# Moving scale chains, statistics, inversions and negations behind an emptied matmul bank in a fused attention and SwiGLU kernel

## The chip, the cores and the metric

One NeuronCore of a Trainium2 chip. Its engines are named as in the profile: PE (TensorE matmul; PEld is its weight load), DVE (VectorE), ACT (ScalarE), POOL (GpSimd) and SP (SyncE, which here issues most of the DMAs). The metric is the device time of one execution in microseconds (us), lower is better. For the kernel before, three runs gave a median of 825.03 us (824.76 to 825.77).

## The reference

```
xn = layernorm(x)                                   # x is 2048 x 512, no gain or bias
q, k, v = split(xn @ wqkv)                          # 32 heads of 16
scores = q k^T * 16**-0.5, masked to 0 <= i - j < 256
s = softmax(scores) v @ wo                          # attention in a sliding window
h = silu(xn @ w1) * (xn @ w3)                       # 512 -> 1792
g = silu(h @ w2)                                    # 1792 -> 512
out = x + s * g
```

All inputs and the output are f32.

## The kernel before, in words

Each f32 matrix is held as a high and a low f16 part, and a product is three matmuls (high by high, high by low, low by high). The tokens are worked in 4 tiles of 512 (t), the heads in 4 groups of 8 (g), and a group in two halves (p): 32 **units** (t, g, p). Each unit goes over its scores twice. `pass1` forms scores (L637) only for the row maxima, which DVE takes together with the mask (L651). `negate` (L663, L664) turns the maxima of a unit into a negated high and low part, `finish` has PE transpose them (L670), DVE copies them (L676) and two DMAs put them as extra rows beside the queries (L680). `pass2` forms the scores transposed (L717), DVE adds the mask (L724), ACT takes the exponential (L727), and PE multiplies with the values (L745), whose extra columns give the row sums. The result is copied out of its bank by DVE (L760, L761).

`normalise` ends a head group. The sums come back through DRAM as a 128 x 32 tile `dr` (L782). `invert`, queued 12 steps later, takes the reciprocal (L786), multiplies by a scale (L787), sends it to DRAM (L789) and spreads it with eight DMAs to the 128 rows of `rb` (L793); POOL multiplies `on` by `rb` (L325 is the line of the helper that does POOL's products and differences in two halves of 256 columns). `cut`, 26 steps after `normalise`, has ACT copy the high part (L799) and POOL subtract the low one (L325). These parts are the left operand of the output projection.

The feed-forward is cut into dense pieces: projections of q and k (L581, ACT copies the high part at L590, DVE forms the low one at L594) and of v (L551), gate and up (L918, ACT's tanh L933, DVE L937 and L942, ACT L947, POOL L325), down (L968, emptied by L987, L989 or L992), and the output step `total` (L1019, with ACT L1013 and DVE L1014 ahead of it, DVE L1023 behind it and the store L1028), which for the last 128 tokens is `total_by_columns` (ACT L1041, DVE L1042, PE L1048, DVE L1050 and L1051, stores L1052).

**What sets the order.** PE's order is the program's: it is written out by hand. The other engines are ordered when the kernel is built, by a scheduler that estimates times; `urgent()` raises an operation's priority, and `tc.issue_after(x)` puts what is issued inside it behind instruction x. A step follows each batch of attention work and each dense piece with a cost; `later(n, f)` runs f n steps on. `lasts["emptied"]` is the last DVE operation so far that emptied a matmul bank (L594, L937, L942, L989, L992, L1023); two such banks (m) alternate. `lasts["maximum"]` is the last L651.

A token tile's statistics (L425, L426), its inverse deviation (POOL L451 to L460) and its centring (L463) are a list `behind` of pieces; one of them is taken at the end of each batch that also has a pass1 ahead of it. Scales of weight matrices come from sums of squares (ACT L235 and L876) by a short chain of DVE and PE operations; `then` (L307) queues the last part of such a chain.

Of the kernel before, what the change touches and what calls it, by code (L numbers as in the profile page):

```python
# [15 lines left out]
ALU = mybir.AluOpType  # L16
# [63 lines left out]
def tile_block(ctx: ExitStack, tc: tile.TileContext, x, wqkv, wo, w1, w3, w2, out):  # L80
    nc = tc.nc
# [27 lines left out]
    def take(dtype):  # L109
        free.sort()  # L110
        slot = free.pop(0)[2]
        made = fpool.tile([P, 512 if dtype == F32 else 1024], dtype, name=slot, tag=slot, bufs=1)
        held[id(made)] = slot, made
        return made
# [19 lines left out]
    def urgent():  # L134


        return tc.high_priority(offset=200) if started else nullcontext()
    made_so_far = [0]

    def later(n, f):  # L140
        made_so_far[0] += 1
        queue.append((now[0] + n, made_so_far[0], f))
# [21 lines left out]
    def scores_bank():  # L164

        return pss.tile([P, 2, 512], F32, name="s")
# [9 lines left out]
    behind = []  # L176
# [116 lines left out]
    def then(s, read, *made):  # L293

        first, *rest = *(read if isinstance(read, tuple) else (read,)), *made

        def chain():
            for f in rest:
                f()

        def behind_bank():
            with tc.issue_after(lasts["emptied"].ins) if "emptied" in lasts else nullcontext():
                chain()

        def now_and_later():
            first()
            later(2, behind_bank)  # L307
        if s is not None:
            return now_and_later
        first()  # L310
        chain()
# [10 lines left out]
    def halves(op, out, a, b):  # L322

        for c in (slice(0, 256), slice(256, 512)):
            op(out[:, c], a[:, c], b[:, c])  # L325
# [83 lines left out]
    lasts = {}  # L409
# [150 lines left out]
    sc = {}  # L560

    def keys(t, g):
        return KA[(t * NG + g) % 3]
# [55 lines left out]
    def pass1(t, g, p):  # L619


        M = small.tile([P, 2, 2, 4], F32, name="M")
        whole = NM[(2 * (t * NG + g) + p) % len(NM)]
        nm = whole[:, 0:32].rearrange("p (b i) -> p b i", b=2)

        def part(ii, a, beside, narrow):
            qa, ka = QA[t, g], keys(t, g)
            i = t * 4 + ii
            n, mask = ((i + 1) * P, M1.rearrange("p a b -> p (a b)")[:, (1 - i) * P:]) if i < 2 else (WIN, MW)
            s = pso.tile([P, 2, TW], F32, name="po") if beside else scores_bank()  # L630

            w = 32 if narrow else 64
            for c in range(0, P, w):
                e = (ii + 3) * P if i < 2 else (ii + 2) * P + 64 * (c // 64 + 1)
                for r in range(2):
                    rows = slice(64 * r, 64 * r + KR)
                    nc.tensor.matmul(s[c:c + w, r, :n], qa[rows, 2 * p + a, ii * P + c:ii * P + c + w],  # L637
                                     ka[rows, 2 * p + a, e - n:e], start=True, stop=True)
            after = []
            if narrow:  # L640
                pass
            elif alone[0] and maxima and (ii, a) != (0, 0):
                after = [f(s) for f in maxima]
                maxima.clear()
            elif alone[0] and besides:
                after = [besides.pop(0)(s)]
            alone[0] = not after or t * NG + g <= 2
            for r in range(2):
                junk = ppool.tile([P, D], BF16, name="junk", bufs=1)
                with urgent():  # L650
                    lasts["maximum"] = nc.vector.tensor_tensor_reduce(  # L651
                        out=junk[:, :n], in0=s[:, r, :n], in1=mask, scale=1.0,
                        scalar=NEG, op0=ALU.add, op1=ALU.max, accum_out=M[:, r, a, ii:ii + 1])
            if (ii, a) == (3, 1):
                later(2, negate)
                maxima.append(finish)
            for f in after:
                f()

        def negate():  # L660
            Mf = M.rearrange("p r a i -> p (r a i)")
            with tc.issue_after(lasts["emptied"].ins):
                nc.vector.tensor_scalar(nm[:, 0, :], Mf, -1.0 / ONE, None, op0=ALU.mult)  # L663
                nc.vector.scalar_tensor_tensor(nm[:, 1, :], Mf, -1.0 / ONE, nm[:, 0, :], op0=ALU.mult, op1=ALU.subtract)  # L664

        def finish(s):

            for h in range(2):
                rows = slice(64 * h, 64 * h + 64)
                nc.tensor.matmul(s[0:64, h, 448:512], whole[rows, 0:64], identh[rows, rows], start=True, stop=True)  # L670

            def rest():
                qa = QA[t, g]
                mt = small.tile([32, P], F16, name="mt")
                with urgent():
                    nc.vector.tensor_copy(mt.rearrange("p (h q) -> p h q", h=2), s[0:32, :, 448:512])  # L676
                dm = dpool.tile([32, P], F16, name="dm")
                nc.sync.dma_start(dm, mt)
                for r in range(2):
                    nc.sync.dma_start(qa[64 * r + KR:64 * r + KR + 2, 2 * p:2 * p + 2, :].rearrange("p a q -> p (a q)"),  # L680
                                      dm.rearrange("(b r i) q -> r b (i q)", b=2, r=2)[r])
            return rest
        return [lambda *kind, ii=ii, a=a: part(ii, a, *kind) for ii in range(4) for a in range(2)]

    def last_maxima():
# [93 lines left out]
    def normalise(t, g):  # L779
        on, dd = ON.pop((t, g))  # L780
        dr = small.tile([P, 32], F32, name="dr")
        nc.sync.dma_start(dr, dd.rearrange("h (b c) -> (h b) c", c=32))  # L782
        rb = opool.tile([P, TW], F32, name="rb", bufs=1)

        def invert():
            nc.vector.reciprocal(dr, dr)  # L786
            nc.vector.tensor_scalar(dr, dr, sc["o"], None, op0=ALU.mult)  # L787
            de = dpool.tile([8, TW], F32, name="de")
            nc.sync.dma_start(de.rearrange("h (b c) -> (h b) c", c=32), dr)  # L789
            for i in range(8):  # L790
                p, r, a = i // 4, i // 2 % 2, i % 2
                h = r * 4 + 2 * p + a
                nc.sync.dma_start(rb[16 * h:16 * h + 16, :], de[i:i + 1, :].to_broadcast([16, TW]))  # L793
            halves(nc.gpsimd.tensor_mul, on, on, rb)

        def cut():
            OT[t, g] = made = take(F16)
            O[t, g] = o = made.rearrange("p (a q) -> p a q", a=2)
            nc.scalar.copy(o[:, 0, :], on)  # L799
            halves(nc.gpsimd.tensor_sub, o[:, 1, :], on, o[:, 0, :])  # L800
        later(12, invert)
        later(26, cut)
# [292 lines left out]
    units = [(t, g, p) for t, g in tiles for p in range(2)]  # L1095
# [18 lines left out]
    def more(want):  # L1114

        made = []
        while ffn and (done[0] < want or ffn[0][0] == 0 or is_open(made)):
# [10 lines left out]
    LAST_PLANS = ((("LW", ()), ("WW", ()), ("WW", ()), ("", (0, 1, 2, 3, 4))),  # L1128
                  (("WW", ()), ("WW", ()), ("W", ()), ("", (0, 1, 2, 3, 4))))

    def batches(n, u, ahead):

        rows1 = pass1(*ahead) if ahead else []
        rows2, cols = pass2(*u) if u else ([], None)
        plan = AHEAD_PLAN if not u else LAST_PLANS[n - len(units) + 2] if not ahead else PLAN if u[0] else FIRST_PLAN
        made = []
        for kinds, cs in plan:
            rows = []
            for k in kinds:
                if k == "W":  # L1140
                    rows.append(rows2.pop(0))
                elif k == "L":
                    rows.append(last_maxima)
                else:
                    rows.append(lambda f=rows1.pop(0), k=k: f(k == "X", k == "N"))

            def batch(rows=rows, cs=cs):
                alone[0] = True
                for f in rows:
                    f()  # L1150
                if cs:
                    cols(*cs)
                if behind and ahead:
                    with tc.issue_after(lasts["maximum"].ins):
                        behind.pop(0)()
            made.append((COLS * len(cs), batch))
        assert not rows1 and not rows2
        return made
# [112 lines left out]
    beside_scores(4, lambda s: then(s, qk[2][2](s), lambda: later(1, qk[2][3])))  # L1271
    later(6, qk[3][1])
    spread(batches(-2, None, units[0]), value(2) + value(3) + more(EARLY // 2))
    beside_scores(3, lambda s: then(s, qk[3][2](s), lambda: later(2, qk[3][3])))
    spread(batches(-1, None, units[1]), project(0, 2, 1) + project(0, 2, 0) + more(EARLY))
# [8 lines left out]
    for n in range(len(units)):  # L1284
        t = n // 8
# [67 lines left out]
```

## Time and profile before

| | |
|---|---|
| median of three runs | 825.03 us (824.76 to 825.77) |
| the profiled execution's own time | 823.93 us |
| its span, first to last instruction | 822.1 us |
| mean granted TensorE clock | 0.999 |
| instructions | 22902 |
| DVE's waits for its DMA at L786 | 9.5 us in 6 |

A line of a timeline gives the start in us, the duration in us, the engine, the line of the kernel, the operation, what it writes and reads, and, in brackets, how long the engine stood idle ahead of it and what ended that. A line of the waits gives the engine and tile that waited, what it waited for, the total in us, how often, and the longest one. In a row of the windows, the busy time and count of PE, PEld, DVE, ACT and POOL follow the window's length, then come the granted clock, the share of the DMA engines and GB/s.

### The profile page before, as it was taken

To read this page: it belongs to the slowest core of one execution; us is meant where nothing else is said; L and a number is where in the kernel's file an instruction comes from. 1 tells how busy PE (TensorE), PEld (TensorE's weight loads), DVE (VectorE), ACT (ScalarE), POOL (GpSimd) and SP (SyncE) were. 2 spreads that over 40 slices of the span, in tenths; PEclk is the share of its full clock that TensorE was granted. 3 is DMA by queue.
4 is the path that set the end of the run, shared out by engine and by line. 5 is a ranking of instruction groups with operands and counts; after the bars stand their busy time and mean duration, and the time that the engine had idled before them with its cause. 6 is when DMAs were issued, how large, how long until landed. Compare 5 with 4: busy or idle time off the path is not lost. (4 is left out here: it accounts for less than half of the span.)

```text
span 822.1 us, 22902 instructions
## 1 busy us (share of the span) xinstructions
PE 802.3 (98%) x8924; PEld 380.1 (46%) x8924; DVE 633.5 (77%) x2021; ACT 389.4 (47%) x562; POOL 205.9 (25%) x355
## 2 busy tenths in 40 slices
PE   8999999999999999999999999999999999999998
PEld 4444444444444444444445444444444444444444
DVE  8787788888787588878878876877777787776435
ACT  6889785645345344243343444442433344432511
POOL 2237274342203113021211112120202022030301
PEclk9999999999999999999999999999999999999999
DMA  9987656157442444544434334534434343332101
GB/s 283 251 252 236 208 176 203 63 148 242 126 134 78 120 131 126 153 124 134 136 94 131 99 89 144 136 121 121 129 82 143 105 112 116 108 121 86 52 22 53
DMA packets 95326, 110.66 MB, mean 135 GB/s; under 512 B 17200, under 2 KB 60528, under 8 KB 95216
## 3 DMA queue, kind: packets, MB, share of 16 engines
q1 hardware_dynamic: 94928, 108.67, 45.3%
q8 instruction: 70, 1.15, 0.6%
q10 hardware_dynamic: 288, 0.52, 0.2%
q14 instruction: 40, 0.33, 0.1%
HBM read 76.28 MB, written 28.57 MB: 128 GB/s over the span
## 5 line engine op out<-in xcount | busy, mean ns | idle before, releaser
L325 POOL TENSOR_TENSOR slot<-slot,slot 128x256 f16<-128x256 f32 (+1 forms) x228 | 151.5, 691 | 518.5 <-ACT slot L947 391.9
L918 PE MATMUL m<-XH,slot 128*128 128x512 f16 x896 | 267.3, 380 | 3.1 <-DVE slot L937 1.7
L727 ACT ACTIVATE pt<-s,es 128x1024 f32<-128x1024 f32 x152 | 167.7, 1113 | 194.4 <-DVE s L724 192.5
L918 PEld LDWEIGHTS <-slot 128*128 128x128 f16 x1344 | 125.1, 98 | 158.1 <-issue 14.0
L918 PE MATMUL m<-XL,slot 128*128 128x512 f16 x448 | 169.8, 379 | 0.0
L968 PE MATMUL m<-slot,slot 128*128 128x512 f16 x672 | 156.6, 380 | 1.8 <-DVE slot L594 0.7
L724 DVE TENSOR_TENSOR s<-s,MK 128x256 f32<-128x256 f32 (+2 forms) x280 | 118.4, 435 | 49.5 <-PE s L717 47.1
L651 DVE CUSTOM_DVE_ANT_0 junk<-s,MW 128x320 bf16<-128x320 f32 x276 | 134.1, 486 | 24.3 <-PE s L637 15.8
L968 PEld LDWEIGHTS <-slot 128*128 128x128 f16 x672 | 61.9, 98 | 80.4 <-issue 9.9
L651 DVE CUSTOM_DVE_ANT_0 junk<-po,MW 128x320 bf16<-128x320 f32 x172 | 83.6, 486 | 5.1 <-DVE mt L676 0.3
L745 PE MATMUL po<-pt,V 64*32 64x320 f32 (+4 forms) x2880 | 77.2, 342 | 0.0
L947 ACT CAST slot<-slot 128x512 f16<-128x512 f32 x56 | 34.5, 617 | 73.4 <-DVE slot L942 68.7
L933 ACT ACTIVATE slot<-m,sgs 128x512 f32<-128x512 f32 x56 | 38.3, 684 | 56.8 <-PE m L918 56.8
L745 PEld LDWEIGHTS po<-pt,V 64*32 64x32 f32 x2880 | 51.0, 106 | 21.4 <-issue 0.8
L717 PE MATMUL s<-qa,KA 50*64 50x320 f16 (+3 forms) x1472 | 58.2, 259 | 1.2 <-ACT pt L727 0.6
L937 DVE SCALAR_TENSOR_TENSOR slot<-slot,m 128x512 f32<-128x512 f32 x56 | 38.3, 685 | 23.4 <-ACT slot L933 23.2
L717 PEld LDWEIGHTS <-KA 50*64 50x64 f16 x1472 | 30.2, 105 | 55.6 <-issue 34.0
L637 PE MATMUL s<-KA,qa 48*64 48x320 f16 (+3 forms) x824 | 45.4, 294 | 2.9 <-ACT pt L727 1.6
L942 DVE SCALAR_TENSOR_TENSOR slot<-m,slot 128x512 f32<-128x512 f32 x56 | 38.5, 688 | 10.6 <-PE m L918 10.1
L992 DVE SCALAR_TENSOR_TENSOR slot<-m,dsc,slot 128x512 f32<-128x512 f32 x48 | 35.9, 748 | 13.4 <-PE m L968 13.1
L581 PE MATMUL m<-XH,whi 128*128 128x512 f16 x120 | 44.7, 381 | 1.1 <-DVE slot L937 0.7
L581 PE MATMUL m<-XL,whi 128*128 128x512 f16 x120 | 44.5, 379 | 0.0
(162 smaller groups left out, 875.2 us busy)
## 6 DMA issues: line engine op xcount, KB each, us to landing
slot<-dW SPq DMA_DIRECT2D x126, 256.0 KB
slot<-in_B_w_dram SPq DMA_DIRECT2D x42, 256.0 KB
dW<-slot SPq DMA_DIRECT2D x42, 256.0 KB
slot<-in_A_x_dram SPq DMA_DIRECT2D x30, 256.0 KB
KA<-dK SPq DMA_DIRECT2D x24, 288.0 KB
qa<-dQ SPq DMA_DIRECT2D x32, 192.0 KB
dQ<-slot SPq DMA_DIRECT2D x16, 256.0 KB
dK<-slot SPq DMA_DIRECT2D x16, 256.0 KB
```

The source lines that it names most:

```text
L325: op(out[:, c], a[:, c], b[:, c])
L581: nc.tensor.matmul(cell["pp"], a[:, k, c, :], b[:, c, :], start=(c, i) == parts[0][0], stop=(c, i) == parts[-1][-1])
L637: nc.tensor.matmul(s[c:c + w, r, :n], qa[rows, 2 * p + a, ii * P + c:ii * P + c + w], ka[rows, 2 * p + a, e - n:e], start=True, stop=True)
L651: lasts["maximum"] = nc.vector.tensor_tensor_reduce(out=junk[:, :n], in0=s[:, r, :n], in1=mask, scale=1.0, scalar=NEG, op0=ALU.add, op1=AL ...
L717: nc.tensor.matmul(s[64 * h:64 * h + 64, r, o:o + 64 * n], ka[rows, 2 * p + a, 64 * (m + 4):64 * (m + 5)], qa[rows, 2 * p + a, 64 * (m + k ...
L724: nc.vector.tensor_add(v, v, MK[:, kind, of:of + n, :].unsqueeze(1).to_broadcast([P, 2 * len(which), n, 64]))
L727: nc.scalar.activation(pt, s, AF.Exp, scale=es)
L745: nc.tensor.matmul(cell["po"][32 * i:32 * i + 32, h, 64 * (m + k):64 * (m + k + n)], V[64 * h:64 * h + 64, (4 * t + m // 2) % VB, hd * VW: ...
L918: nc.tensor.matmul(cell[k], w[:, (a * NC + c) * P:(a * NC + c + 1) * P], b[:, c, :], start=c == 0 and i == 0, stop=c == NC - 1 and i == 2)
L933: nc.scalar.activation(sg, cell[0], AF.Tanh, scale=sg_scale[:, f:f + 1])
L942: lasts["emptied"] = nc.vector.scalar_tensor_tensor(sg, cell[1], 0.5 * HS / (WS * XS)**2, sg, op0=ALU.mult, op1=ALU.mult)
L968: nc.tensor.matmul(ps, hh[:, a * TW + b * P:a * TW + (b + 1) * P], w[:, c * D:(c + 1) * D], start=f == f0 and i == 0, stop=f == f1 - 1 and ...
```

## The change

Five edits. The last part of a weight's scale chain comes three steps on instead of two. So does the negation of a unit's maxima, but the last unit's is issued at once. The two DVE operations of `invert` are put behind the bank emptied last. The tokens' statistics are no longer put behind the last maximum at the end of their batch; they are queued three steps on and put behind the bank emptied last, by the new `behind_bank`. In the changed kernel, lines from L786 on are numbered one higher, those from `batches` on six and then five.

```diff
         def now_and_later():
             first()
-            later(2, behind_bank)
+            later(3, behind_bank)
...
             if (ii, a) == (3, 1):
-                later(2, negate)
+                later(3, negate) if (t, g, p) != units[-1] else negate()
                 maxima.append(finish)
...
         def invert():
-            nc.vector.reciprocal(dr, dr)
-            nc.vector.tensor_scalar(dr, dr, sc["o"], None, op0=ALU.mult)
+            with tc.issue_after(lasts["emptied"].ins):
+                nc.vector.reciprocal(dr, dr)
+                nc.vector.tensor_scalar(dr, dr, sc["o"], None, op0=ALU.mult)
             de = dpool.tile([8, TW], F32, name="de")
...
+    def behind_bank():
+
+        with tc.issue_after(lasts["emptied"].ins):
+            behind.pop(0)()
+
     def batches(n, u, ahead):
...
                 if behind and ahead:
-                    with tc.issue_after(lasts["maximum"].ins):
-                        behind.pop(0)()
+                    later(3, behind_bank)
             made.append((COLS * len(cs), batch))
```

## The prediction

> **What bounds the kernel now.** I read the page first, then the waits of PE and of DVE, then the timeline around the longest waits and over the last 33 us, and last the granted clock by windows. "Stall" below always means time in which PE starts no matmul. The page gives the span and who fills it:
>
> ```profile
> PE 802.3 (98%) x8924; PEld 380.1 (46%) x8924; DVE 633.5 (77%) x2021; ACT 389.4 (47%) x562; POOL 205.9 (25%) x355
> ```
>
> PE is busy 98% of 822.1 us, and its list of work doesn't change. So all that a reordering can win are PE's stalls, and all that it can lose are new ones. The waits of PE, each with its total, count and longest one, and the waits of DVE:
>
> ```profile
> PE s L670 <- DVE NM L664: 1.8, 3, 1.1
> PE m L918 <- DVE slot L937: 1.7, 3, 0.8
> ```
>
> ```profile
> DVE dr L786 <- DMA dr<-dd: 9.5, 6, 3.5
> ```
>
> The longest single wait of PE is for the negation (L664). The 9.5 us are DVE standing still ahead of `reciprocal` (L786) for its DMA; DVE executes in order, so what is behind L786 stands still too. These two are what edits 2 and 3 of the change touch. A shown gap of PE is smaller than its stall: the last projection's row below has 36 matmuls in 7.93 us, so one starts every (7.93 - 0.38) / 35 = 0.216 us while each is drawn 0.38 long. A stall is the shown gap plus 0.16.
>
> **The change part by part.** The built instruction order of the changed kernel keeps PE's order and moves rows of DVE, ACT, POOL and SP; so the edits do what they say, and I follow the rows that move.
>
> *Gain 1, L786 behind an emptied bank.* All 16 inversions move 3 to 8 us later on DVE. The largest wait, on DVE and then on PE:
>
> ```profile
> 213.85 0.35 DVE L786 RECIPROCAL dr<-dr 128x32 f32<-128x32 f32 x1 [3.54 <-DMA dr<-dd]
> 214.24 0.24 DVE L787 TENSOR_SCALAR dr<-dr,so 128x32 f32<-128x32 f32 x1
> ...
> 214.72 0.68 DVE L937 SCALAR_TENSOR_TENSOR slot<-slot,m 128x512 f32<-128x512 f32 x1
> ```
>
> ```profile
> 215.45 0.59 PE L918 MATMUL m<-XH,slot 128*128 128x512 f16 x2 [0.82 <-DVE slot L937]
> ...
> 217.68 0.33 PE L637 MATMUL s<-KA,qa 48*64 48x320 f16 x4 [0.39 <-DVE XL L511]
> ```
>
> The pair costs 214.24 + 0.24 - 213.85 = 0.63 us of DVE, and the wait before it 3.54. With the pair behind L937, the bank is emptied about 4 us earlier, PE's stall of 0.82 + 0.16 = 0.98 goes, and with DVE ahead by that much so does the next one, 0.39 + 0.16 = 0.55: 1.53 us. Two more waits lie ahead of stalls in the same way:
>
> ```profile
> 258.05 0.35 DVE L786 RECIPROCAL dr<-dr 128x32 f32<-128x32 f32 x1 [1.53 <-DMA dr<-dd]
> ```
>
> ```profile
> 262.84 0.42 PE L717 MATMUL s<-qa,KA 50*64 50x320 f16 x12 [0.33 <-DVE XL L511]
> ```
>
> ```profile
> 710.02 0.35 DVE L786 RECIPROCAL dr<-dr 128x32 f32<-128x32 f32 x1 [1.00 <-DMA dr<-dd]
> ```
>
> ```profile
> 719.80 0.33 PE L637 MATMUL s<-KA,qa 48*32 48x320 f16 x8 [0.68 <-ACT pt L727]
> ```
>
> DVE comes 1.53 us earlier to the first, more than its stall of 0.33 + 0.16 = 0.49; that goes. The second, 0.68 + 0.16 = 0.84, is held by an exponential (L727) that runs behind `tanh` of the output step on ACT; DVE's 1.00 reaches it only by way of POOL and ACT. I take all of it, with nothing as the other end.
>
> *Gain 2, work that the later scales push on.* One 1.18 us `L1014` falls behind two maxima, and PE waits for just those:
>
> ```profile
> 532.74 1.18 DVE L1014 SCALAR_TENSOR_TENSOR slot<-slot,slot 128x512 f32<-128x512 f32 x1
> ```
>
> ```profile
> 534.92 0.33 PE L637 MATMUL po<-KA,qa 48*64 48x320 f16 x4 [0.42 <-DVE M L651]
> ```
>
> The maxima come 1.18 us earlier, the stall of 0.42 + 0.16 = 0.58 goes.
>
> *Gain 3, the last negation at once.* In the last unit it no longer stands behind the two copies out of the score bank and a bank's emptying:
>
> ```profile
> 746.37 0.69 DVE L760 COPY os<-po 128x512 f32<-128x512 f32 x1 [0.24 <-PE po L745]
> 747.09 0.69 DVE L761 TENSOR_TENSOR os<-os,po 128x512 f32<-128x512 f32 x1
> 747.77 0.75 DVE L992 SCALAR_TENSOR_TENSOR slot<-m,dsc,slot 128x512 f32<-128x512 f32 x1
> ...
> 748.63 0.17 DVE L664 SCALAR_TENSOR_TENSOR NM<-M,NM 128x16 f16<-128x16 f32 x1
> ```
>
> ```profile
> 748.86 0.22 PE L670 MATMUL s<-identh,NM 64*64 64x64 f16 x2 [1.14 <-DVE NM L664]
> ```
>
> The three rows ahead of it take 748.4 - 746.4 = 2.0 us; the stall is 1.14 + 0.16 = 1.30 and goes whole. What is late next is L760, by the negation's 0.4 us; L992, the emptying, ends 0.4 later, and PE has the other bank by then. In the other 31 units the negation comes about a step later; PE waits for it three times in all, 1.8 us with the 1.1 of this one (the first row of PE's waits), so there is room in nearly all of them, and I cost this at nothing; were the cover gone, each unit could lose at most the step's emptying, 0.7 us.
>
> *Loss 1, the tokens' statistics.* Behind a bank, they land twice ahead of the second of two maxima, where they stood behind it:
>
> ```profile
> 175.66 0.69 DVE L425 BATCH_NORM_STATS2 st<-slot 128x6 f32<-128x512 f32 x1
> ```
>
> ```profile
> 176.06 1.36 PE L745 MATMUL po<-pt,V 64*32 64x320 f32 x44
> ```
>
> ```profile
> 374.35 0.69 DVE L425 BATCH_NORM_STATS2 st<-slot 128x6 f32<-128x512 f32 x1
> ```
>
> ```profile
> 374.76 0.31 PE L637 MATMUL po<-KA,qa 48*64 48x320 f16 x4
> ```
>
> The maximum ends where L425 starts, plus 0.08 of its read-out; PE needs its bank 0.4 us after, so the slack is 0.33 and the maximum moves 0.69: 0.36 lost at each, 0.72 together.
>
> *Loss 2, the first 150 us.* The scale chains of the weights move there as well, and ACT is the limit:
>
> ```profile
> 60.00:80.00 20.00, 18.70 (x151) 8.37 (x150) 15.87 (x67) 19.97 (x40) 13.58 (x22) 1.00 0.82 253
> ```
>
> ACT is busy 19.97 of 20 us, so what DVE gains ahead of that is not passed on. One row goes the other way: the sum of squares
>
> ```profile
> 95.26 0.63 ACT L876 ACTIVATE sqa<-slot 128x512 bf16<-128x512 f32 x1 [1.25 <-DMA slot<-in_B_w_dram]
> ```
>
> now stands ahead of the exponential at 90.25, for which PE already waits:
>
> ```profile
> 91.39 0.25 PE L637 MATMUL s<-KA,qa 48*64 48x128 f16 x4 [0.19 <-ACT pt L727]
> ```
>
> 0.63 lost, at most; at the other end the 1.25 us that ACT stands idle at 95.26 are used and nothing is lost. I take 0.63.
>
> *Loss 3, the end.* Here the last inversion moves behind two more emptyings and the first L992 of the last tile, and everything that hangs on it moves with it. First DVE, then the issues on SP, then POOL, ACT and PE:
>
> ```profile
> 802.33 0.75 DVE L992 SCALAR_TENSOR_TENSOR slot<-m,dsc,slot 128x512 f32<-128x512 f32 x1 [1.88 <-PE m L968]
> ```
>
> ```profile
> 795.83 0.33 SPq L789 DMA_DIRECT2D de<-dr  x1
> 797.25 3.56 SPq L793 DMA_DIRECT2D rb<-de  x8
> ```
>
> ```profile
> 802.43 1.42 POOL L325 TENSOR_TENSOR on<-on,rb 128x256 f32<-128x256 f32 x2
> 808.43 1.30 POOL L325 TENSOR_TENSOR slot<-on,slot 128x256 f16<-128x256 f32 x2 [4.58 <-ACT slot L799]
> ```
>
> ```profile
> 807.75 0.60 ACT L799 CAST slot<-on 128x512 f16<-128x512 f32 x1
> ```
>
> ```profile
> 807.95 7.93 PE L1019 MATMUL m<-slot,slot 128*128 128x512 f16 x36
> ```
>
> Before, L789 is issued at 795.83, and POOL multiplies from 802.43: at most 6.60 us later, of which 1.42 + 3.56 are the two issues on SP and at most 1.62 the last landing. After: L992 ends at 803.05, the pair takes 0.63, L789 goes out at 803.70, POOL starts by 810.30 and is done 1.42 later, L799 runs 811.75 to 812.35, and POOL's first half of the low part (0.65) to 813.05. PE needs the high part of the fourth head group for its 10th matmul, 807.95 + 9 x 0.216 = 809.89, and the low part for the 12th, 810.33. It gets them at 812.35 and 813.05: a stall of 2.46, then 0.26 more, 2.7 in all; 2.3 if the last landing takes 1.2 instead of 1.62, and 3.6 if the eight issues are slowed by the outputs. I take 2.6. Nothing comes after this stage that could give it back: the rest of PE's work and the last stores follow the projection.
>
> **The sum.** Gains 1.53 + 0.49 + 0.84 + 0.58 + 1.30 = 4.74; losses 0.72 + 0.63 + 2.6 = 3.95; net -0.8 us. Against the profiled execution (823.93 us, its span 822.1 and 1.8 around it) that is 823.1; the median of the runs shown, 825.03, lies 1.10 higher, so the number for it is **824.2**.
>
> **The rivals.**
>
> *A, faster: the end costs little or the gains run on.* If DVE, ahead by 9.5 us of removed waits, also clears some of the short stalls that I left alone, or the last landing is short, the gains reach 5.9 and the end 2.3: net -2.2, 822.8. With the end free altogether it would be 4.74 - 1.35 = -3.4, 821.6. For it: DVE is 77% busy and its waits are the ones removed. Against it: the rows of the end leave only 809.89 - 808.35 = 1.5 us of slack for a chain that moves by 7.9.
>
> *B, slower: the stalls come back one matmul on.* The removed DVE wait pays only if L937 and the scores' split find their own inputs earlier. If ACT's `tanh` or the DMA of the next operand is what ends last once L786 is gone, PE stops at the next bank instead, and only the two stalls remain won whose cause is plain order, 0.58 + 1.30. Then 3.95 - 1.88 = +2.1: 827.1. It decides once less than 2.3 of the 4.74 is kept. For it, ACT too has waits that later inversions lengthen:
>
> ```profile
> ACT slot L799 <- POOL on L325: 29.0, 11, 4.2
> ```
>
> Against it: ACT is busy only 47% of the span, and its busiest stretch, 60 to 80 us, lies ahead of the first of these 11 waits.
>
> *C, the clock.* The stall at the end lets PE rest 2.5 us. The granted clock (the third column from the right) against PE's work (the second):
>
> ```profile
> 818.00:820.00 2.00, 0.51 (x5) 0.20 (x3) 1.16 (x3) 0.00 (x0) 0.00 (x0) 1.00 0.55 197
> 820.00:822.00 2.00, 0.00 (x0) 0.00 (x0) 0.00 (x0) 0.00 (x0) 0.00 (x0) 0.65 0.20 70
> ```
>
> PE is done at 818.5; a mean of 0.65 is full speed for 0.6 us and half for 1.4, so the clock fell at 820.6, 2.1 us after the last matmul. A stall of 2.5 could meet that. Seen at half clock are 1.4 us, worth 0.7 of matmul time; all 8.3 us left after the stall at half clock would cost 8.3. Taken near the short end, 1.7: net +0.9, 825.9. The Trainium skill ("TensorE: Matmul & The Clock Gate", Part 1) says that the clock halves after at least one idle window of about 3.4 us, windows running free of the kernel. By it a rest of 2.5 us would leave the clock full, and the time would be the forecast's; the trace's 2.1 us is shorter than such a window, so the row doesn't bear the figure out, and I keep the rival.
>
> **How the numbers follow.** A measurement of this kernel can tell about 0.2%, 1.65 us, from no change. Forecast as summed, 0.40, and C, 0.05, both within that; A 0.30, faster; B 0.25, slower. The range takes in A with the end free (821.6) and B (827.1): 821.5 to 827.2, and leaves out C's far end and gains beyond A.
>
> **What would show it.** Right: DVE's waits lose `dr L786 <- DMA`; PE's stalls near 215, 262, 534 and 748 are gone; new ones stand near 176 and 374, a longer one near 91; the last L786 starts at 803 and the row of 36 matmuls is split by about 2.6 us after the ninth. Wrong: no split there (then A), or new PE waits for L937, L942 or L727 between 215 and 720 that add up to more than 2 us (then B), or a granted clock under 1.00 between 812 and 818 (then C).

## The result and the profile after

The changed kernel takes 833.58 us, median of 5 runs (832.85 to 834.35), against 825.40 (824.76 to 826.56, 5 runs) before: a ratio of 1.0098 with a 95% interval of 1.0083 to 1.0113, or 8.2 us slower. The forecast was 824.2 and its range ended at 827.2.

The profiled execution after took 834.35 us, its span is 832.6. It lies 0.8 above its median and that of before 1.5 below its own, so the two traces are 10.4 us apart. Lines from L786 on are numbered one higher. From the page and from the waits of PE, of DVE and of ACT after:

```profile
PE 803.8 (97%) x8924; PEld 380.8 (46%) x8924; DVE 626.9 (75%) x2021; ACT 387.6 (47%) x562; POOL 205.9 (25%) x355
```

```profile
PE s L637 <- ACT pt L727: 5.0, 5, 2.3
PE m L919 <- DVE slot L938: 3.4, 4, 1.8
PE s L717 <- ACT pt L727: 3.0, 3, 1.9
PE m L1020 <- ACT slot L800: 2.7, 1, 2.7
```

```profile
DVE dr L787 <- DMA dr<-dd: 1.0, 1, 1.0
```

```profile
ACT slot L800 <- POOL on L325: 66.6, 16, 8.7
```

The reader is to see a wait that changed its engine. DVE's waits for the sums fell from 9.5 us to 1.0, as intended. ACT's waits for POOL's product rose from 29.0 us in 11 to 66.6 in 16, and two of PE's four largest waits are now for the exponential, which runs on ACT.

PE's order is the same in both kernels, so its matmuls can be laid side by side one by one. The time by which the changed kernel is late grows or shrinks only at stalls (changes of 0.25 us and more, gathered by place; places are times of before):

| place | forecast | measured |
|---|---|---|
| start to 150 us | +0.63 | +3.07 |
| 150 to 190 | +0.36 | +1.48 |
| 215 and 217 | -1.53 | -1.36 |
| 231 | 0 | +1.89 |
| 262 | -0.49 | -0.55 |
| 374 | +0.36 | none |
| 476 | 0 | +0.82 |
| 534 | -0.58 | -0.53 |
| 546 | 0 | +1.90 |
| 719 | -0.84 | none |
| 748 | -1.30 | -1.15 |
| the end, stall | +2.6 | +3.15 |
| the end, half clock | rival C | +1.70 |
| sum | -0.8 | +10.4 |

The end, from the combined timeline after:

```profile
808.57 0.34 DVE L787 RECIPROCAL dr<-dr 128x32 f32<-128x32 f32 x1
...
810.64 3.97 SPq L794 DMA_DIRECT2D rb<-de  x8
...
813.53 2.11 PE L1020 MATMUL m<-slot,slot 128*128 128x512 f16 x9
...
816.19 1.40 POOL L325 TENSOR_TENSOR on<-on,rb 128x256 f32<-128x256 f32 x2 [8.15 <-DMA rb<-de]
817.63 0.62 ACT L800 CAST slot<-on 128x512 f16<-128x512 f32 x1 [2.09 <-POOL on L325]
818.30 8.00 PE L1020 MATMUL m<-slot,slot 128*128 128x512 f16 x27 [2.67 <-ACT slot L800]
```

The row of 36 matmuls is split into 9 and 27, where the prediction split it. The windows of the same stretch (busy us and count of PE, PEld, DVE, ACT and POOL, then the granted clock):

```profile
816.00:818.00 2.00, 0.00 (x0) 0.00 (x0) 0.27 (x1) 0.37 (x1) 1.40 (x2) 1.00 0.00 0
818.00:820.00 2.00, 1.56 (x6) 0.57 (x7) 0.52 (x1) 0.25 (x1) 1.29 (x2) 0.90 0.00 0
820.00:822.00 2.00, 2.00 (x7) 0.66 (x5) 0.92 (x2) 0.00 (x0) 0.00 (x0) 0.50 0.11 34
822.00:824.00 2.00, 2.00 (x9) 0.81 (x8) 0.25 (x1) 0.00 (x0) 0.00 (x0) 0.75 0.29 106
```

PE starts again at 818.30 at full rate, and about 1.3 us later the clock halves: 0.4 us of the second row, all of the third and 1.0 us of the fourth, 3.4 us, which cost 1.7. The third row has seven matmuls, where the row from 812 to 814 us, at full clock, has eleven.

At 546 the wait stands on ACT, then on DVE, then on PE (three views of after, ACT, DVE and PE):

```profile
551.13 0.62 ACT L800 CAST slot<-on 128x512 f16<-128x512 f32 x1 [7.99 <-POOL on L325]
551.66 0.68 ACT L934 ACTIVATE slot<-m,sgs 128x512 f32<-128x512 f32 x1
```

```profile
552.37 0.69 DVE L938 SCALAR_TENSOR_TENSOR slot<-slot,m 128x512 f32<-128x512 f32 x1 [3.03 <-ACT slot L934]
```

```profile
553.11 0.59 PE L919 MATMUL m<-XH,slot 128*128 128x512 f16 x2 [1.76 <-DVE slot L938]
```

ACT stood idle for 8 us with `tanh` (L934) behind the cast of the attention's output. The inversion had ended at 530.53 before and ends at 539.02 now, 8.5 us later, of which 4.8 are the delay of everything there. At 231 it is the same with an exponential (L727) behind the cast: ACT stood idle for 8.70 us, and PE then shows a gap of 1.87.

### The profile page after: what moved, and what is told of

Same layout as the page of the kernel before. It is cut to its first block, busy times and chain, and to the rows that moved or that the text cites. A ratio compares the mean times of both kernels' runs of the same rounds, so it can differ in the third digit from the quotient of the medians.

```text
span 832.6 us, 22904 instructions
## 1 busy us (share of the span) xinstructions
PE 803.8 (97%) x8924; PEld 380.8 (46%) x8924; DVE 626.9 (75%) x2021; ACT 387.6 (47%) x562; POOL 205.9 (25%) x355
## 3 DMA queue, kind: packets, MB, share of 16 engines
q8 instruction: 70, 1.15, 0.6%
## 5 line engine op out<-in xcount | busy, mean ns | idle before, releaser
L727 ACT ACTIVATE pt<-s,es 128x1024 f32<-128x1024 f32 x152 | 167.4, 1112 | 172.5 <-DVE s L724 169.2
L969 PE MATMUL m<-slot,slot 128*128 128x512 f16 x672 | 156.6, 380 | 2.2 <-DVE slot L943 0.9
L934 ACT ACTIVATE slot<-m,sgs 128x512 f32<-128x512 f32 x56 | 38.2, 682 | 49.3 <-PE m L919 49.2
L1020 PE MATMUL m<-slot,slot 128*128 128x512 f16 x180 | 43.9, 391 | 2.8 <-ACT slot L800 2.7
```

Of the source, the lines that this page charges most:

```text
L727: nc.scalar.activation(pt, s, AF.Exp, scale=es)
L969: nc.tensor.matmul(ps, hh[:, a * TW + b * P:a * TW + (b + 1) * P], w[:, c * D:(c + 1) * D], start=f == f0 and i == 0, stop=f == f1 - 1 and ...
L1020: nc.tensor.matmul(ps, O[t, g][:, a, tb], w[g], start=g == 0 and i == 0, stop=g == NG - 1 and i == 2)
```

## The experiments

Theory after the result: the later inversion delays POOL's product, and what stands in order behind that product on ACT (the cast, then L727 or L934) stops PE in the middle of the kernel as well as at the end; and the first 150 us are lost to the scale chains. The rival: the losses in the middle come from DVE's new order, whichever edit makes it. All kernels are compared with the kernel before, whose median was 825.7 to 826.0 beside them; each had 4 to 12 runs. A difference in us is worked out from the measured ratio, which is not exactly the quotient of the two medians.

**E1, the inversion alone.**

```diff
         def invert():
-            nc.vector.reciprocal(dr, dr)
-            nc.vector.tensor_scalar(dr, dr, sc["o"], None, op0=ALU.mult)
+            with tc.issue_after(lasts["emptied"].ins):
+                nc.vector.reciprocal(dr, dr)
+                nc.vector.tensor_scalar(dr, dr, sc["o"], None, op0=ALU.mult)
```

> Only the inversion behind an emptied bank. Theory: this edit carries the losses at 231 and 546 us (1.9 each, exponential and tanh standing behind the cast of L799 that waits for POOL), 0.7 near 184, and the end (3.1 of stall and 1.7 of halved clock), less the stalls won at 215 to 218 and 262 (1.9): about +7.4 us on the kernel before, 832 to 833. Rival: the losses at 231 and 546 come from the other edits' moves on DVE, and this edit alone is the end less the stalls won: +2.9, about 828.

Measured 834.87 us, ratio 1.0109 (1.0088 to 1.0129), +9.0. Laid beside before, its matmuls gain 0.99 and 0.59 at 215 and 217, 0.55 at 262 and 0.53 at 534, and lose 2.02 and 0.62 at 184 to 187, 1.88 at 546, 3.15 at the end and 1.7 to the clock. The traced run was the fastest of the five, 832.29 us, and 8.4 behind before's trace. Its ACT waits 65.5 us for POOL's product. So this one edit is as dear as the whole change; the single edits, E1 to E4, add up to +10.8 us against its 8.2, and the intervals don't say whether that differs. The 231 stall, 1.9 in the whole change, is only 0.3 here: against PE the cast comes 1.6 us earlier, and the exponential behind it almost in time. Which of the other edits makes up the difference was not tested.

**E2, the scale chains alone.**

```diff
-            later(2, behind_bank)
+            later(3, behind_bank)
```

> Only the scale chains one step later. Theory: the exponential at 91 us behind more sums of squares (2.0) and the stall at 112 (1.2) are this edit's: +2.5 to +3.1 us, about 828. Rival: as in the prediction, the early moves nearly balance: within +-0.7 of the kernel before.

Measured 829.31 us, ratio 1.0043 (1.0028 to 1.0058), +3.5: the theory. It loses 1.2 at 68, 1.9 at 91 and 1.1 at 112, and wins 0.7 at 112 and 0.7 at 215. ACT of this run around 68, and PE (the reader is to look at the brackets):

```profile
62.54 1.33 ACT L328 ACTIVATE slot<-slot,pi 128x512 f32<-128x512 f32 x2 [0.52 <-DVE pi L288]
...
67.70 0.72 ACT L328 ACTIVATE slot<-slot,sw 128x512 f32<-128x512 f32 x1 [0.66 <-DVE sw L894]
68.33 0.67 ACT L933 ACTIVATE slot<-m,sgs 128x512 f32<-128x512 f32 x1
```

```profile
69.83 0.59 PE L918 MATMUL m<-XH,slot 128*128 128x512 f16 x2 [1.56 <-DVE slot L937]
```

A scaling of weights (L328) waits for its scale, 0.52 and 0.66 us, and `tanh` behind it comes late. Work that ACT didn't do then is still there at 91, ahead of the exponential. There one more thing comes on top. The sum of squares that the prediction saw move ahead of the exponential brings the wait for its weight's DMA with it, 0.63 us in E2. In the changed kernel it is 0.74, on ACT and then on PE:

```profile
92.14 0.63 ACT L877 ACTIVATE sqa<-slot 128x512 bf16<-128x512 f32 x1 [0.74 <-DMA slot<-in_B_w_dram]
...
92.77 1.09 ACT L727 ACTIVATE pt<-s,es 128x1024 f32<-128x1024 f32 x1
```

```profile
93.92 0.25 PE L637 MATMUL s<-KA,qa 48*64 48x128 f16 x4 [2.30 <-ACT pt L727]
```

**E3, the statistics alone.**

```diff
-                    with tc.issue_after(lasts["maximum"].ins):
-                        behind.pop(0)()
+                    later(3, behind_bank)
```

> Only the tokens' statistics three steps later and behind an emptied bank. Theory: 0.4 to 0.6 lost near 176 and no more, +0.5 us in all. Rival: the statistics also delay what centres the tokens, and the stalls of +0.7 near 150 and +0.4 near 164 are theirs: +1.5 to +2 us.

Measured 826.18 us, ratio 1.0005 (0.9995 to 1.0015), +0.4: the theory, though the interval doesn't part it from no change. The stall at 176 is there, 0.24.

**E4, the last negation alone.**

```diff
-                later(2, negate)
+                later(2, negate) if (t, g, p) != units[-1] else negate()
```

> Only the last unit's negation at once, the others two steps on as before. Theory: the stall of 1.3 us at 748 goes and stays won: -1.2 us. Rival: the copies of the score bank that now come 0.4 us later stop PE, and 0.4 or less is left of it.

Measured 823.77 us, ratio 0.9975 (0.9965 to 0.9985), -2.1. Faster, as the theory says, by 1.2 to 2.9 us; its trace wins 1.2 at 748, and the rest of the 2.1 stands at no place of it that this edit touches. DVE, then PE, of this run:

```profile
746.17 0.18 DVE L664 SCALAR_TENSOR_TENSOR NM<-M,NM 128x16 f16<-128x16 f32 x1
746.44 0.69 DVE L760 COPY os<-po 128x512 f32<-128x512 f32 x1
```

```profile
747.45 0.22 PE L670 MATMUL s<-identh,NM 64*64 64x64 f16 x2
```

No bracket is left at the transposes. This kernel differs from before in the order of five DVE instructions at 746 us and nowhere else, and yet its trace has 0.7 us more at 112 and 0.8 less at 215: so much does a single place vary between executions. At 215 this bears on gain 1. E3 and E6, which leave the inversion as before too, are 0.74 and 0.53 shorter there. So 0.5 to 0.8 of the 0.98 that the prediction read at 215 stood in the one trace of before and not in these. In E4 DVE waits 2.77 us for the sums there instead of 3.54, and PE has no bracket:

```profile
215.06 0.59 PE L918 MATMUL m<-XH,slot 128*128 128x512 f16 x2
```

**E5 and E6, the cast on POOL.** ACT then has nothing in its row that waits for POOL's product; E5 with the inversion of E1, E6 without.

```diff
         def cut():
...
-            nc.scalar.copy(o[:, 0, :], on)
+            if (t, g) != tiles[-1]:
+                for c in (slice(0, 256), slice(256, 512)):
+                    nc.gpsimd.tensor_copy(o[:, 0, c], on[:, c])
+            else:
+                nc.scalar.copy(o[:, 0, :], on)
```

> Only the inversion behind an emptied bank, and the cast of the high part (ACT L799) runs on POOL in two halves, in all head groups but the last; ACT then has nothing that waits for POOL's product. Theory (ACT stands behind that cast): the stalls of 2.0 and 0.6 near 187 and of 1.9 near 549 of the run with the inversion alone are gone, the end stays as it is (+4.9): +3 to +4.5 us on the kernel before, 829 to 830.5. Rival (the inversion's place on DVE or the queues of the DMAs make these stalls): they stay, +7.5 to +9.5.

> The kernel before with the cast of the high part on POOL in all head groups but the last, nothing else changed: the control of the run beside it. Theory: ACT's 29 us of waits at L799 cost PE nothing before, so within +-1 us of the kernel before. Rival: they cost already, -1.5 to -3; or POOL's longer queue (1.3 us more in each group) stops the feed-forward, +1 to +3.

E6 measured 825.91 us, ratio 0.9997 (0.9987 to 1.0008): moving the cast costs and wins nothing that the runs can tell (its one trace, of the slowest run, is still 3.0 us longer than before's). E5 measured 832.45 us, ratio 1.0082 (1.0065 to 1.0099), +6.8, between the two expectations. In its trace the 546 stall is gone, as the theory wants; and since DVE's order in E5 is that of E1, instruction for instruction, DVE's order alone does not make that stall, as the rival would have it. The stall at 187 isn't gone; it has another way. POOL, DVE and PE of E5:

```profile
185.59 1.41 POOL L325 TENSOR_TENSOR on<-on,rb 128x256 f32<-128x256 f32 x2 [12.39 <-DMA rb<-de]
186.94 0.74 POOL L802 CAST slot<-on 128x256 f16<-128x256 f32 x2
187.64 1.30 POOL L325 TENSOR_TENSOR slot<-on,slot 128x256 f16<-128x256 f32 x2
188.90 0.20 POOL L451 TENSOR_TENSOR sq<-r 128x4 f32<-128x4 f32 x1
...
191.48 0.20 POOL L460 TENSOR_TENSOR rs<-sq,r 128x4 f32<-128x4 f32 x1
```

```profile
191.71 0.55 DVE L463 TENSOR_SCALAR slot<-slot,mv,rs 128x512 f32<-128x512 f32 x1 [3.61 <-POOL rs L460]
192.17 0.68 DVE L594 SCALAR_TENSOR_TENSOR slot<-m,slot 128x512 f16<-128x512 f32 x1
```

```profile
192.91 1.01 PE L923 MATMUL m<-XH,slot 128*128 128x512 f16 x2 [3.40 <-DVE slot L594]
```

POOL waits 12.39 us for `rb`, in order behind it stand the ten small steps of a tile's inverse deviation, DVE stands 3.61 us at the centring that needs them, and the emptying of a bank stands behind that. The late `rb` finds whichever engine has its reader in the row.

**E7, the last inversion as before.**

```diff
         def invert():
-            with tc.issue_after(lasts["emptied"].ins):
+            with tc.issue_after(lasts["emptied"].ins) if (t, g) != tiles[-1] else nullcontext():
```

> Only the inversion behind an emptied bank, but the last head group's one as before. Theory: the end's stall (3.1) and the half clock after it (1.7) are gone and the clock is 0.999 to 1.000 in every run; what stays is the middle: +3 to +4 us, 829 to 830. Rival: the clock falls for other stalls as well, so that runs at 0.996 remain: +5 to +6.

Measured 828.51 us, ratio 1.0041 (1.0024 to 1.0057), +3.4: the end is about 5.6 of the 9.0 by these ratios, stall and clock together, and 4.85 in E1's trace; E7's trace has neither. In that the theory holds. That the clock stays full does not: in this trace PE shows a gap of 3.21 us near 187, and the clock falls after it (windows of E7):

```profile
186.00:188.00 2.00, 0.00 (x0) 0.00 (x0) 0.00 (x0) 1.12 (x2) 1.27 (x3) 1.00 0.64 159
188.00:190.00 2.00, 1.43 (x16) 0.72 (x16) 1.12 (x7) 1.03 (x2) 1.74 (x7) 1.00 0.00 0
190.00:192.00 2.00, 2.00 (x6) 0.68 (x5) 1.08 (x6) 1.15 (x2) 1.08 (x6) 0.52 0.22 49
192.00:194.00 2.00, 2.00 (x7) 0.80 (x6) 0.67 (x2) 0.00 (x0) 0.00 (x0) 0.63 0.53 176
```

Up to 800 us E7 has the same instruction order on DVE, ACT and POOL as E1, where the gap near 187 is only 1.85. What differs is when SP, which issues in order too, gets a DMA out. Before, `de` of this head group, (0, 1), went out ahead of a load of keys (`KA`) that still waited; with the inversion later it stands behind that load, and `rb` behind both. SP before, then SP of E1:

```profile
169.57 0.34 SPq L789 DMA_DIRECT2D de<-dr  x1
173.33 0.32 SPq L613 DMA_DIRECT2D KA<-dK  x1
173.71 3.93 SPq L793 DMA_DIRECT2D rb<-de  x8
```

```profile
173.21 0.32 SPq L613 DMA_DIRECT2D KA<-dK  x1
173.58 0.44 SPq L790 DMA_DIRECT2D de<-dr  x1
...
177.07 4.90 SPq L794 DMA_DIRECT2D rb<-de  x8
```

From the inversion's end to the issue of `de` it is 0.5 us in the changed kernel, 2.1 in E1 and 3.4 in E7, and PE's gap near 187 is 0.50, 1.85 and 3.21. In these three traces the stall follows that delay; why the load goes later in one execution than in another is not shown.

**E8 to E10, only what wins.** E8 is E4 with the inversion of E7 and the cast of E6. E9 is E8 with the inversion of head group (0, 1) as before too. E10 is E4 with the inversions of (0, 1), (2, 1) and the last as before and the cast on ACT.

```diff
-            with tc.issue_after(lasts["emptied"].ins) if (t, g) != tiles[-1] else nullcontext():
+            with tc.issue_after(lasts["emptied"].ins) if (t, g) not in ((0, 1), (3, 3)) else nullcontext():
```

> The last negation at once, the inversions but the last behind an emptied bank, and the cast of the high part on POOL in all head groups but the last. Theory: the stalls won by the inversion (1.6 near 215, 0.5 near 262, 0.5 near 535) and the negation (1.2 to 2.1) add up and nothing is lost: -3 to -4.5 us, 821.5 to 823. Rival: the waits won come back elsewhere: no better than the negation alone, about -2.

> As the run with negation, inversions and the cast on POOL, but the inversion of head group (0, 1) is left as before as well as the last one. Theory (the 187 us stall of 2.7 there came from POOL's product for that one group, behind which POOL's reciprocal root and DVE's centring stood, and halved the clock): the stall and its 1.6 us of half clock are gone, -3 to -4 us on the kernel before, about 822.5. Rival: the stall comes from the cast on POOL alone; it stays, and the time is -0.5 as before.

> The last negation at once, and the inversions behind an emptied bank in all head groups but (0, 1), (2, 1) and the last; the cast stays on ACT. Theory: these three groups carry every loss of the inversion, the stalls won at 215, 217 and 262 (2.1 in all) add to the negation's: -3 to -4 us, about 822.5. Rival: the waits come back at other groups: no better than the negation alone, -2.

E8: 825.38 us, ratio 0.9996 (0.9984 to 1.0009), where -3 to -4.5 was expected; its trace has the 187 stall, 2.7, with 1.6 of half clock behind it, and wins 0.98 and 0.59 at 215 and 217, 0.59 at 262, 0.49 at 534 and 1.16 at 748. E9: 822.96 us, ratio 0.9969 (0.9957 to 0.9980), -2.6, and the 187 stall is gone: it was that one head group. E10: 823.12 us, ratio 0.9971 (0.9962 to 0.9979), -2.4. With the cast still on ACT, its trace has no stall at 187, 231, 546 or the end, and the 0.42 at 534 is back: those at 534 and 546 both come with the inversion of (2, 1). Both kernels fall short of the 3 to 4 us expected. Both beat before and after, but their intervals overlap E4's: that the inversion's wins (2.7 us in the trace of E9, 2.1 in that of E10) add to the negation's isn't shown, and 0.8 us of them, at 215, are in E4's trace as well. Both traces also lose 0.6 at 149.8; E12's does without that edit, so it isn't the inversion's for certain.

**E11, the whole change without the inversion.** The changed kernel with `invert` as before.

> The changed kernel without its edit of the inversion. Theory: the three other edits add up, +3.5 for the scales, +0.4 for the statistics, -2.1 for the last negation: +1.8 us on the kernel before, about 827.5; no half clock. Rival: the edits interact, and without the inversion the kernel is level with before or faster: 0 to -2.

Measured 828.90 us, ratio 1.0037 (1.0023 to 1.0051), +3.1; the +1.8 of the theory lies just below the interval's 1.9. The negation and the scales don't interact in the kernel's favour. The theory had no half clock in it; four of the five runs have a mean clock of 0.996 to 0.998.

**E12, the scales four steps on.**

```diff
-            later(2, behind_bank)
+            later(4, behind_bank)
```

> Only the scale chains, four steps on instead of two (the change has three). Theory (ACT, which works without a gap there, stands in order behind a scaling that waits for its scale): a further step adds about as much as the first, +5 to +7 us on the kernel before. Rival: the loss at three steps is an accident of where the sums of squares fell: +1 to +4, no more than at three steps.

Measured 838.01 us, ratio 1.0155 (1.0141 to 1.0169), +12.8: the direction of the theory and twice its size. The rival is out. The same 30 us of before, E2 and E12, where the fourth pair is ACT's:

```profile
60.00:90.00 30.00, 28.70 (x274) 13.26 (x273) 22.49 (x89) 29.65 (x61) 19.51 (x31) 1.00 0.84 271
```

```profile
60.00:90.00 30.00, 27.50 (x269) 12.90 (x268) 21.43 (x83) 28.60 (x57) 19.42 (x31) 1.00 0.80 253
```

```profile
60.00:90.00 30.00, 25.22 (x216) 10.66 (x222) 19.45 (x74) 26.09 (x50) 19.12 (x30) 0.94 0.70 227
```

With two, three and four steps ACT is busy 29.65, 28.60 and 26.09 us of 30, and PE 28.70, 27.50 and 25.22. What ACT loses there, PE loses too. That ACT loses it to a missing scale is shown for E2 alone, by the two brackets above. In E12 ACT's one long gap of this stretch is for the DMA of a weight, and why that comes late is not shown:

```profile
64.55 0.63 ACT L876 ACTIVATE sqa<-slot 128x512 bf16<-128x512 f32 x1 [3.07 <-DMA slot<-in_B_w_dram]
```

## Why the prediction was wrong, point by point

- **The step that failed: the inversions in the middle, costed at nothing.** Under gain 1 the prediction moved all 16 inversions 3 to 8 us back and then stopped following L786. It followed the chain L789, L793, POOL, L799 only for the last one, under loss 3, and in the middle put the move at nothing. E1 shows 2.6 near 187 and 1.9 at 546; the whole change shows 0.7 near 187, 1.9 at 231 and 1.9 at 546. These 4.5 us are the largest part of the 11.2 between the forecast sum (-0.8) and the traces (+10.4). E5 shows that the 546 stall goes when ACT has no reader of POOL's product in its row, E10 that it goes when the inversion of (2, 1) stays where it was, and E9 the same of the 187 stall and (0, 1). The row was there: ACT already waited 29.0 us at L799, up to 4.2 at once, which says that in 11 of 16 cases ACT had nothing left to do ahead of this chain's end. The prediction quoted it, under rival B, and set no price on it. The row doesn't say which of them PE feels: of the 16 moved inversions, those of (0, 1), (0, 2), (2, 1) and the last one stopped PE.
- **Gain 1 itself** came in size: 1.58 at 215 and 217 and 0.55 at 262 in E1 (forecast 1.53 and 0.49). At 215 that was partly luck, because 0.5 to 0.8 of it is missing in kernels that leave the inversion alone (E3, E4, E6). The 0.84 at 719 did not come: PE's gap is 0.67 or 0.68 there in every trace.
- **Gain 2** came, 0.53 of 0.58, but from another edit: E1 alone has it and E2 alone has not. It is the inversion, not a later scale, that makes the stall go; in E10, with the inversion of (2, 1) as before, the stall is back.
- **Gain 3** came, 1.15 of 1.30.
- **Loss 1** was of the right size at 176, 0.24 in E3 and 0.57 in the whole change (forecast 0.36); at 374 it is 0.11 in both.
- **Loss 2, the second step that failed.** From ACT at 19.97 of 20 us the prediction concluded that DVE's gains aren't passed on, and took 0.63, "at most". It did not ask what a late scale does to an engine that has no idle time to make up for it: E2's ACT waits 0.52 and 0.66 us for scales, with `tanh` in order behind, and PE loses 1.2. And it took the 1.25 us for which ACT waited at the sum of squares as time to be used, where the wait moved along with that row, 0.74 of it, ahead of the exponential. The first 150 us lose 3.07 in the whole change; E2 measured 3.5, E12 12.8.
- **Loss 3** was right: 2.7 worked out, 2.6 taken, 3.15 measured, by the same chain (L787 started 13.4 us later than before, 7.8 of them more than the rest; the prediction had 7.9).
- **Rival C** came as told, 1.7 us, on top of the stall that the forecast had, and in other kernels not only at the end; the mean clock of all five runs is 0.996 to 0.998. By the prediction's own row (2.1 us) the stall of 2.5 was long enough, so 0.05 was a small chance for it. The Trainium skill ("TensorE: Matmul & The Clock Gate", Part 1) has the clock halve after at least one idle window of about 3.4 us; here a stall of 2.8 was enough, so that condition isn't borne out, while the 3.4 us at half clock are one such window long.
- **Rival B** had the right sign and the right row, but its mechanism (the stalls come back one matmul on) isn't what happened: the stalls that were to go went.

Left open: why `rb` is issued 3.7 us after `de` at 546 and not 1.4 as at the end; why the whole change has the stall at 231 and E1 hardly any; and the 0.8 at 476, a place that is 0.2 to 0.5 longer in most of the other traces too, E4's among them, which leaves the order there as it was.

## What to carry to other kernels

A step moved back is to be followed to its last reader at every one of its places, not only at the last one; an engine that already waits for that chain's end is the sign that there is no slack. SP's DMA issues stand in order as well: near 187 the `de` that fell behind a waiting load took over up to 3.4 us of that load's wait. The price of a wait is not its length: here 9.5 us of waiting on DVE cost PE about 2, and the 37.6 us more on ACT that took their place cost 4.5 in the middle and 4.9 with the clock at the end. What counts is what stands in order behind the wait, and whether PE needs it by then. And where one engine has no idle time, as ACT here from 60 to 90 us, an input that comes late is not made up for. Last, one trace of before is one execution: a stall that is to be won should be seen in a second trace.

## What the runs showed of the hardware

The granted clock falls after rests of PE of 2 to 3 us in these traces, and not always. It halved for about 3.4 us after a gap of 2.67 us at the end of the changed kernel, and after 3.21 in E7; in E1 a gap of 1.85 near 187 left it at 1.00. The changed kernel itself has a gap of 2.30 at 93.92, and the clock stays (its windows):

```profile
92.00:94.00 2.00, 0.08 (x5) 0.08 (x8) 0.11 (x1) 1.72 (x3) 0.00 (x0) 1.00 0.47 152
94.00:96.00 2.00, 2.00 (x19) 0.93 (x19) 1.72 (x10) 1.16 (x2) 0.00 (x0) 1.00 0.00 0
```

In E11 a gap of 2.01 at 95.08 was enough to halve it, and so were, near 31 us, shown gaps of 1.27 and 0.64 close together (windows of E11):

```profile
30.00:32.00 2.00, 0.58 (x12) 0.38 (x12) 0.45 (x4) 2.00 (x5) 0.00 (x0) 0.93 1.10 344
32.00:34.00 2.00, 2.00 (x12) 0.67 (x6) 1.52 (x9) 2.00 (x5) 1.26 (x3) 0.50 0.79 236
34.00:36.00 2.00, 2.00 (x8) 0.74 (x7) 1.90 (x7) 1.44 (x3) 2.00 (x4) 0.72 1.12 232
```

PE is busy 0.58 of 2 us in the first of these rows, and then 3.4 us pass at half clock. So the length of the gap alone doesn't decide it here: 2.01 us halved the clock and 2.30 did not. Executions of one kernel differ too: E7's mean clock was 1.000 in three runs of 826.8 to 828.1 us and 0.997 to 0.998 in four of 828.5 to 830.5 (one of these four has a trace). Half clock for 3.4 us costs 1.7; a stall of 2 us or more may cost that on top.
